# The fifth product of four pairs of steps of a feed-forward layer, computed as seven smaller products and added to its sum by POOL

## The chip, the cores and the metric

The kernel runs on one core of a Trainium2 chip. The metric is the device time of one execution in microseconds; the kernel before took 848.61 us in the median of three runs (847.42 to 848.70).

## The reference

The program computes an attention whose mask comes from hash buckets of the queries and keys, and then a feed-forward block on its output. The change is in the first layer of that block, `h = x @ w_in`:

```python
n_tokens, d_model, d_ff = (3072, 512, 2048)

def _moe_ref(x, w_in, w_out) -> np.ndarray:
    h = x @ w_in
    g = h * (1.0 / (1.0 + np.exp(-1.702 * h)))
    return (g @ w_out).astype(np.float32)
```

## The kernel before

**The tiling.** x is held transposed (`xT`), so the first layer's output has d_ff on the partitions. The layer is computed by Strassen's scheme in Winograd's form: instead of eight products of quarters there are seven, of sums of quarters. `quarters_in` gives the seven left factors (quarters of w_in and their sums in `s_in`), `quarters_x` the seven right ones (quarters of x and their sums in `t_x`); `LEFT` and `RIGHT` say which belong to products 1 to 7. A step takes 128 rows of each half of d_ff and a block of 1,024 tokens (`sb`, three of them). Each of its seven products has 128 x 256 times 256 x 512, two matmuls of 512 columns; eight steps make a block, 24 the layer. In the trace each such fp32 matmul is two records.

**Pairs.** Steps 2 to 21 run in pairs t = 1 to 10 (`pair_of_steps(t)`, steps 2t and 2t+1; t // 4 is the block). Two steps together give a product of 256 x 256 times 256 x 512, which can be split by the same scheme once more ("nested"): seven matmuls of 128 x 128 times 128 x 256 take the place of four of 512 columns. Before the change this is done for products 2, 4 and 3 (`TWICE`), and products 1, 6, 5 and 7 are done whole, as `p1`, `p6`, `p5`, `p7`, once for each of the two steps. `nested` returns five pieces (`one` to `five`, with 1, 2, 1, 2 and 1 of the seven matmuls); each piece leaves a PSUM half bank (`at`) that DVE then adds into the tile concerned (`into`). The factors of a nested product are sums of sums: `nest_w` makes the left ones, `nest_x` the right ones, all on POOL. The results of the pair stand in four tiles u, v, c21 and c22 of 128 x 1,024. There are two sets of them, one for odd t and one for even t; a new tile of a set takes the place of that of t - 2.

**The order.** PE, DVE, ScalarE (ACT) and POOL each work strictly in the order written out. A pair has eight slots, one for each of its whole products in `order`. Work that is to come later is put down with `plan(t, at, ...)`, for slot `at` of pair t (from 9 on: slot `at - 8` of the next pair, from 17 on of the one after), and `play` brings it behind the slot's product: first what was planned with `small=True` (the pieces of nested products), then the rest. So in every slot the pieces come first. Product 2's pieces into u are planned from slot 3, product 3's into v from slot 4 (its second piece in slot 6), product 4's into c21 from slot 9 (its fourth and fifth pieces in slots 7 and 8 of the next pair).

**What else is planned.** `g_part`: four sums of the second layer's input (lines 230 to 233) on POOL, in slots 12, 13, 14 and 17; the last reads c21 and c22. `todo`: the conversion of w_out from its 64-bit form, in six steps on DVE (L188, L190, L196, L201, L205, L208), with a square on ACT (L198) and a load on ACT's queue; two steps each in slots 2, 3 and 4 for step 2t, two each in slots 6 and 7, one in 8 and one in 9 for step 2t+1, as far as there are conversions. `low`: the sums over a part of w_out in the last pair, t = 10, three on POOL (L222, L224, L225) and one on DVE (L223), which overwrites what the first one reads. Product 5 before the change: `p5(i)` is a product of two matmuls into the bank "b", added to v by DVE (L919) and copied to c22 by ACT (L1035); `p7(i)` goes on in the bank of `p1` and `p6`, and DVE adds it to c22 (L919), ACT copies it to c21 (L1040). There are two banks "a", one for each step of a pair; the next pair's first product needs the first of them.

Of the kernel before, what the change touches and what calls it, by code (L numbers as in the profile page):

```python
# [38 lines left out]
def kernel(  # L39
# [806 lines left out]
    def feed_forward(tag, late=()):  # L846
# [9 lines left out]
        with ExitStack() as fctx:  # L856
# [75 lines left out]
            X = {}  # L932
            TWICE = (2, 4, 3)

            def nest_w(t):
                sums = {}
                m = slice(2 * t * P, (2 * t + 2) * P)
                for o in TWICE:
# [3 lines left out]
                    new = w_out_sb[:, t - 2, 12:16, :] if (o, n) == (4, 4) else nest.tile([P, n, P], F32, name=f"w{o}{t}")  # L942
                    new = [new[:, i] for i in range(n)]
                    s3 = x[2] if n == 3 else new[3]
                    W[o, t] = [x[0], x[1], s3, x[3]] + new[0:3]
                    sums[o] = sums_a(nc.gpsimd, x[0], x[1], s3, x[3], *new[0:3], a21=x[2])
                return sums

            def nest_x(sb, rooms):
                sums = {}  # L950
                rooms = list(rooms)
                for o in (2, 3, 4):
# [4 lines left out]
                    sums[o] = [lambda a=t1, b=b12, c=b11: nc.gpsimd.tensor_tensor(a, b, c, op=Alu.subtract),  # L957
                               lambda a=t2, b=b22, c=t1: nc.gpsimd.tensor_tensor(a, b, c, op=Alu.subtract),
                               lambda a=d12, b=b22, c=b12: nc.gpsimd.tensor_tensor(a, b, c, op=Alu.subtract),
                               lambda a=t4, b=b21, c=t2: nc.gpsimd.tensor_tensor(a, b, c, op=Alu.subtract)]  # L960
                return sums

            def nested(o, sb, t, tiles, name, bank_of, done):
# [10 lines left out]
                def into(x, first):  # L974
                    dst = tiles[name][:, first * TH : first * TH + x.shape[-1]]
                    add(dst, x, dst)

                def one():
                    ps[0] = bank_of()
                    into(go(1, True), 0)  # L980

                def two():
                    go(6)
                    go(2)
                    into(ps[0], 0)

                def three():
                    into(go(7), 3)

                def four():  # L990

                    x, y = go(4), go(5, True)
                    into(x, 2)
                    into(y, 3)

                def five():
# [15 lines left out]
            def pair_of_steps(t):  # L1012

                sb, m0 = divmod(2 * t, MT)
                tiles, a = {}, [None, None]

                def place(name, i):
                    if name not in tiles:
# [10 lines left out]
                    nc.scalar.copy(place("v", i), a[i])  # L1029

                def p5(i):
                    b = outer_bank("b")
                    product(b, sb, m0 + i, 5)
                    add(place("v", i), b, place("v", i))
                    nc.scalar.copy(place("c22", i), b)  # L1035

                def p7(i):
                    product(a[i], sb, m0 + i, 7, False)
                    add(place("c22", i), a[i], place("c22", i))
                    nc.scalar.copy(place("c21", i), a[i])  # L1040
                    if i:
                        emit(tiles["c22"])
                        keep(sb, m0, 3, tiles["c22"], nc.scalar)

                def done(at):
                    def f(x):
# [20 lines left out]
                for i, at in enumerate((12, 13, 14, 17)):  # L1067
                    for j in range(2):
                        plan(t, at + j, lambda i=i, j=j: g_part(i, j))
                order = (p1, 0), (p1, 1), (p6, 0), (p5, 0), (p6, 1), (p5, 1), (p7, 0), (p7, 1)  # L1070
                for at, (f, i) in enumerate(order, 1):
                    f(i)
                    play(8 * t + at)
# [241 lines left out]
            for f in in_sums(1) + in_sums(2, 2):  # L1315
# [23 lines left out]
            for i in (list(range(1, LATE + 1)) if late else []) + free[:FC]:  # L1339
# [20 lines left out]
            for t in NESTED:  # L1360
# [171 lines left out]
```

## Time and profile before

| | us |
|---|---|
| median of three runs | 848.61 |
| the profiled execution | 848.2 |
| its span, first to last instruction | 846.4 |
| PE busy | 836.6 |
| DVE busy | 676.1 |
| POOL busy | 382.8 |
| ACT busy | 337.7 |

The attention runs to 308 us, the first layer to 585 us, the second to the end. Rows of the trace in order of time have the start, the duration, the engine, the line, the operation, what is written and read, and how many records were merged; in brackets stands how long the engine had been idle and what released it. A row of a window has the window, then the busy time of PE, weight loads, DVE, ACT and POOL with counts, the granted clock, and the share and rate of the DMA engines. A row of groups has the number of instructions, their busy time, the mean in ns of one, and the idle time before them.

### The profile page before, as it was taken

The page shows a single profiled execution, that of the slowest core. Times are in us where ns is not written, and L with a number is a line of the kernel's source. Part 1 is how long each engine was busy: PE and PEld are TensorE (multiplying, and loading weights), DVE is VectorE, ACT ScalarE, POOL GpSimd, SP SyncE. Part 2 cuts the span into 40 slices and gives each one's busy share as a digit, 9 for nine tenths or more (in the row PEclk, how much of TensorE's full clock was granted, in tenths as well). Part 3 has the DMA queues.
Part 4 walks back from the last instruction along what each step waited for, and adds up shares of the span by engine and source line. Part 5 has one row for each costly group of instructions (what it writes and reads, how often), then busy time and mean ns, then how long its engine had stood idle before and what let it go on. Part 6 is the DMA issues. An engine that isn't in the chain of part 4 may idle for free.

```text
span 846.4 us, 14968 instructions
## 1 busy us (share of the span) xinstructions
PE 836.6 (99%) x5662; PEld 522.3 (62%) x5662; DVE 676.1 (80%) x1073; ACT 337.7 (40%) x550; POOL 382.8 (45%) x324
## 2 busy tenths in 40 slices
PE   8999999999999999999999999999999999999996
PEld 4444444444444444556666666656888888888885
DVE  6478988887888985785878678848999977797776
ACT  6766766766676634434444344443000000000000
POOL 5433443344344359999844686858865000000000
PEclk9999999999999999999999999999999999999999
DMA  8678887788763105446555546657844685467524
GB/s 142 117 150 142 151 171 132 139 158 153 163 155 96 50 2 173 149 145 229 209 195 199 218 174 224 223 224 249 314 178 166 199 261 199 154 195 249 198 100 101
DMA packets 165341, 144.92 MB, mean 171 GB/s; under 512 B 124112, under 2 KB 140112, under 8 KB 160272
## 3 DMA queue, kind: packets, MB, share of 16 engines
q1 hardware_dynamic: 154352, 110.54, 47.7%
q10 hardware_dynamic: 10912, 33.39, 12.1%
q8 instruction: 45, 0.74, 0.4%
q14 instruction: 32, 0.26, 0.1%
HBM read 79.69 MB, written 50.33 MB: 154 GB/s over the span
## 4 chain that ended last, share of the span: by engine, by line
PE 96%; DVE 2%; issue 1%; POOL 1%; POOLq 0%; DVEq 0%
PE product L1240 28%; PE product L901 22%; PE s L547 15%; PE s L514 15%; PE small L971 7%; PE product L971 4%; PE s L496 2%; PE s L460 1%; PE s L569 1%; DVE t_x L1245 0%; DVE y L1220 0%; DVE t1b L230 0%; DVE raw_g L231 0%; DVE t2b L232 0%; PE s L410 0%
## 5 line engine op out<-in xcount | busy, mean ns | idle before, releaser
L484 ACT ACTIVATE e<-s 128x768 f32<-128x768 f32 x192 | 143.3, 811 | 49.2 <-PE s L514 44.3
L547 PE MATMUL s<-e,v 128*32 128x385 f32 x1536 | 130.9, 488 | 0.0
L525 POOL TENSOR_TENSOR t_x<-e 128x768 f32<-128x768 f32 x32 | 61.1, 1910 | 136.1 <-ACT e L484 121.6
L901 PE MATMUL product<-xT,w_in_sb 128*128 128x512 f32 x208 | 96.8, 592 | 0.0
L547 PEld LDWEIGHTS s<-e,v 128*32 128x32 f32 x1536 | 46.7, 109 | 79.3 <-issue 62.8
L901 PE MATMUL product<-t_x,s_in 128*128 128x512 f32 x192 | 89.8, 593 | 0.0
L514 PE MATMUL s<-s_in 32*128 32x384 f32 x912 | 87.9, 481 | 0.0
L525 POOL TENSOR_TENSOR t_x<-t_x,e 128x768 f32<-128x768 f32 x32 | 55.3, 1727 | 43.3 <-ACT e L484 41.8
L538 DVE TENSOR_TENSOR acc<-acc,e 128x768 f32<-128x768 f32 x63 | 70.9, 1126 | 2.3
L1276 ACT COPY wide<-product 128x256 f32<-128x256 f32 x20 | 7.4, 372 | 158.2 <-PE product L1240 125.0
L901 PEld LDWEIGHTS product<-xT,w_in_sb 128*128 128x128 f32 x208 | 39.4, 190 | 31.8 <-issue 28.9
L514 PEld LDWEIGHTS s<-s_in 32*128 32x128 f32 x912 | 43.9, 185 | 23.3 <-issue 2.2
L901 PEld LDWEIGHTS product<-t_x,s_in 128*128 128x128 f32 x192 | 36.4, 190 | 28.3 <-issue 25.6
L919 DVE TENSOR_TENSOR u<-product,u 128x256 f32<-128x256 f32 (+1 forms) x64 | 29.8, 478 | 23.2 <-PE product L971 20.9
L514 PE MATMUL s<-own 32*128 32x384 f32 x432 | 44.3, 482 | 0.0
L465 DVE TENSOR_SCALAR f<-s,above,weight 128x384 bf16<-128x384 f32 x15 | 10.1, 676 | 36.5 <-PE s L569 23.6
L230 POOL TENSOR_TENSOR u<-v,u 128x1024 f32<-128x1024 f32 (+1 forms) x12 | 26.2, 2182 | 20.8 <-ACT v L916 15.6
L919 DVE TENSOR_TENSOR c<-small,c 128x256 f32<-128x256 f32 (+1 forms) x60 | 26.9, 461 | 9.7 <-PE small L971 9.5
L535 DVE SCALAR_TENSOR_TENSOR acc<-t_x,e 128x768 f32<-128x768 f32 x31 | 29.3, 945 | 6.3 <-POOL t_x L525 3.5
L919 DVE TENSOR_TENSOR v<-small,v 128x256 f32<-128x256 f32 (+1 forms) x60 | 27.1, 466 | 8.5 <-PE small L971 6.0
L1035 ACT COPY c<-product 128x512 f32<-128x512 f32 x20 | 11.7, 586 | 51.9 <-DVE v L919 44.8
L1240 PE MATMUL product<-s_in,xT 128*128 128x256 f32 x136 | 31.3, 379 | 0.0
(302 smaller groups left out, 1808.8 us busy)
## 6 DMA issues: line engine op xcount, KB each, us to landing
raw_g<-g_dram SPq DMA_DIRECT2D x20, 1024.0 KB, 6.1
s_in<-g_dram SPq DMA_DIRECT2D x18, 1024.0 KB, 5.1
g_dram<-c ACTq DMA_DIRECT2D x20, 512.0 KB, 3.1
raw<-in_moe_w_out_dram ACTq DMA_DIRECT2D x16, 512.0 KB, 3.7
raw<-in_moe_w_in_dram ACTq DMA_DIRECT2D x15, 512.0 KB, 5.8
s_in<-own SPq DMA_DIRECT2D x36, 192.0 KB, 4.7
v<-in_v_dram SPq DMA_DIRECT2D x16, 384.0 KB, 4.2
g_dram<-u ACTq DMA_DIRECT2D x10, 512.0 KB, 2.9
```

What stands on the lines that cost most here:

```text
L230: return [lambda: eng.tensor_tensor(t1, b12, b11, op=Alu.subtract), lambda: eng.tensor_tensor(b12, b22, b12, op=Alu.subtract), lambda: eng ...
L484: nc.scalar.activation(es[c][:, kt, :, 0:HS], ps[:, :, 0:HS], Act.Exp, scale=1.0 / D**0.5)
L496: nc.tensor.matmul(ps[:, j, 0:HS], a[hs, keys], m[hs, cols], start=at == 0, stop=at == 1)
L514: nc.tensor.matmul(ps[i][:, j, 0:HS], a[r0 : r0 + 32, keys], m[r0 : r0 + 32, cols], start=at == 0, stop=at == 2)
L525: nc.gpsimd.tensor_tensor(low_sum, low_sum if i else e[:, 0], e[:, i + 1], op=Alu.add)
L535: nc.vector.scalar_tensor_tensor(acc, terms[0], T * TINY, terms[1], op0=Alu.add, op1=Alu.add)
L538: nc.vector.tensor_tensor(acc, acc, terms[i + 1], op=Alu.add)
L547: nc.tensor.matmul(av[D * j + d : D * j + d + 32, :], vt[:, j, row, d : d + 32], es[c][:, t, j, :], start=(t == 0), stop=(t == T - 1))
L901: nc.tensor.matmul(ps, wq[LEFT[i]][:, kc, :], xq[RIGHT[i]][:, kc, :], start=(start and kc == 0), stop=(kc == K2 - 1), skip_group_check=not ...
L919: nc.vector.tensor_tensor(dst, x, y, op=Alu.add)
L971: nc.tensor.matmul(x, wq[LEFT[i]], xq[RIGHT[i]], start=start, stop=True, skip_group_check=True)
L1240: nc.tensor.matmul(ps, wq[LEFT[i]][:, c, :], gq[RIGHT[i]][:, c, :], start=(onto is None and c == 0), stop=(c == F4 - 1), skip_group_check= ...
```

## The change

For t = 5, 6, 9 and 10 (`FIFTH`) product 5 is nested as well. Its first contributions are copied to c22 by ACT (`begin`), the others added by DVE; when all five pieces are through, POOL adds c22 to v, at the head of slot 5's other work. `order` changes, the addition of product 7 to c22 and the gelu and store of c22 come out of `p7` as `p8` and `p9` and stand at the end of slots 7 and 8. The factors get places: the sums of w in a part of w_out's tile, copied from there to `xT` by ACT in pair 8; the sums of x in `xT`, where one place of `spare` (the last g sum's result of pair 5) gives way. The four sums of `low` go to other slots.

```diff
-            def nest_w(t):
+            FIFTH = (5, 6, 9, 10)
+
+            def nest_w(t, which=TWICE):
...
+                    if o == 5:
+                        new = fifth_w[t][0]
...
-            def nest_x(sb, rooms):
+            def nest_x(sb, rooms, which=(2, 3, 4)):
...
+                def begin(x, at):
+
+                    if o == 5:
+                        nc.scalar.copy(tiles[name][:, at * TH : (at + 1) * TH], x)
+                    else:
+                        into(x, at)
+
                 def one():
+                    if name not in tiles:
+                        tiles[name] = staged_pair(name, t % 2 == 1)
                     ps[0] = bank_of()
-                    into(go(1, True), 0)
+                    begin(go(1, True), 0)
 
                 def two():
                     go(6)
                     go(2)
-                    into(ps[0], 0)
+                    if o == 5:
+                        into(ps[0][:, 0:TH], 0)
+                        begin(ps[0][:, TH:], 1)
+                    else:
+                        into(ps[0], 0)
 
                 def three():
-                    into(go(7), 3)
+                    begin(go(7), 3)
 
                 def four():
 
                     x, y = go(4), go(5, True)
-                    into(x, 2)
+                    begin(x, 2)
                     into(y, 3)
...
                 def p5(i):
+                    if fifth:
+                        return
...
                 def p7(i):
                     product(a[i], sb, m0 + i, 7, False)
+                    if not fifth:
+                        p8(i)
+                    nc.scalar.copy(place("c21", i), a[i])
+                    if i and not fifth:
+                        p9()
+
+                def p8(i):
                     add(place("c22", i), a[i], place("c22", i))
-                    nc.scalar.copy(place("c21", i), a[i])
-                    if i:
-                        emit(tiles["c22"])
-                        keep(sb, m0, 3, tiles["c22"], nc.scalar)
+
+                def p9():
+                    emit(tiles["c22"])
+                    keep(sb, m0, 3, tiles["c22"], nc.scalar)
...
+                if fifth:
+                    order = (p1, 0), (p1, 1), (p6, 0), (p6, 1), (p5, 0), (p5, 1), (p7, 0), (p7, 1)
+                    for i, f in enumerate(nested(5, sb, t, tiles, "c22", lambda: outer_bank("b"), lambda x: None), 1):
+                        plan(t, i, f, small=True)
+                    plan(t, 5)
+                    agenda[8 * t + 5][1].insert(0, lambda: nc.gpsimd.tensor_tensor(tiles["v"], tiles["v"], tiles["c22"], op=Alu.add))
+                    plan(t, 7, lambda: p8(0))
+                    plan(t, 8, lambda: p8(1), p9)
...
-                      for k, i in ((3, 0), (2, 0), (3, 0), (3, 1))]
+                      for k, i in ((3, 0), (3, 0), (3, 0), (3, 1))]
...
+            fifth_w = {1: [w_out_sb[:, 0, 12:15, :]], 2: [w_out_sb[:, 0:3, 11, :]]}
+            for i, x in fifth_w.items():
+                x.append(xT[:, i - 1, 2 * XT : 2 * XT + 3 * P].rearrange("p (n d) -> p n d", d=P))
+            fifth_x = {1: [xT[:, 2, i * TH : (i + 1) * TH] for i in range(4)],
+                       2: [xT[:, 2, 2 * j * XT + i * TH : 2 * j * XT + (i + 1) * TH] for j in range(2) for i in range(2)]}
...
+                if t + 1 in FIFTH and (5, t % (MT // 2) + 1) not in W:
+                    plan(t, 7, *nest_w(t % (MT // 2) + 1, (5,))[5])
+                if t in FIFTH and (5, sb) not in X:
+                    agenda.setdefault(8 * t + 1, ([], []))[1][0:0] = nest_x(sb, fifth_x[sb], (5,))[5]
+                if t == MT:
+
+                    for i, (old, new) in fifth_w.items():
+                        plan(t, 1, lambda old=old, new=new: nc.scalar.copy(new, old))
+                        W[5, i][4:] = [new[:, j] for j in range(3)]
                 if t + 1 == NESTED.stop:
-                    for i, f in zip((1, 5, 2, 3), low):
+                    for i, f in zip((6, 8, 7, 8), low):
                         plan(t, i, f)
```

More of the change, by code (lines that the diff above doesn't have):

```diff
@@ L933, in feed_forward @@
             TWICE = (2, 4, 3)
-            def nest_w(t):
+            FIFTH = (5, 6, 9, 10)
+            def nest_w(t, which=TWICE):
                 sums = {}
                 m = slice(2 * t * P, (2 * t + 2) * P)
-                for o in TWICE:
+                for o in which:
                     w = quarters_in(m)[LEFT[o]]
@@ L941, in nest_w @@
                     n = 3 if t < 3 else 4
-                    new = w_out_sb[:, t - 2, 12:16, :] if (o, n) == (4, 4) else nest.tile([P, n, P], F32, name=f"w{o}{t}")
+                    if o == 5:
+                        new = fifth_w[t][0]
+                    else:
+                        new = w_out_sb[:, t - 2, 12:16, :] if (o, n) == (4, 4) else nest.tile([P, n, P], F32, name=f"w{o}{t}")
                     new = [new[:, i] for i in range(n)]
@@ L947, in nest_w @@
                 return sums
-            def nest_x(sb, rooms):
+            def nest_x(sb, rooms, which=(2, 3, 4)):
                 sums = {}
                 rooms = list(rooms)
-                for o in (2, 3, 4):
+                for o in which:
                     b = quarters_x(sb)[RIGHT[o]]
@@ L984, in two @@
                     go(2)
-                    into(ps[0], 0)
+                    if o == 5:
+                        into(ps[0][:, 0:TH], 0)
+                        begin(ps[0][:, TH:], 1)
+                    else:
+                        into(ps[0], 0)
                 def three():
-                    into(go(7), 3)
+                    begin(go(7), 3)
                 def four():
                     x, y = go(4), go(5, True)
-                    into(x, 2)
+                    begin(x, 2)
                     into(y, 3)
@@ L1015, in pair_of_steps @@
                 tiles, a = {}, [None, None]
+                fifth = t in FIFTH
                 def place(name, i):
```

## The prediction

> **What bounds the kernel now.** I read the page first: the busy shares and the chain that ended last.
>
> ```profile
> PE 836.6 (99%) x5662; PEld 522.3 (62%) x5662; DVE 676.1 (80%) x1073; ACT 337.7 (40%) x550; POOL 382.8 (45%) x324
> PE 96%; DVE 2%; issue 1%; POOL 1%; POOLq 0%; DVEq 0%
> ```
>
> TensorE carries nearly the whole chain. A busy PE can still be a waiting one, so next come PE's rows in order of time for the first pair that changes, t=5 ("pair 5"), and the busy time of the stretch behind.
>
> ```profile
> 423.25 0.59 PE L971 MATMUL product<-xT,w 128*128 128x256 f32 x2
> ...
> 427.99 1.88 PE L901 MATMUL product<-t_x,s_in 128*128 128x512 f32 x4
> 429.71 0.59 PE L971 MATMUL small<-xT,s_in 128*128 128x256 f32 x2
> 430.14 1.88 PE L901 MATMUL product<-t_x,s_in 128*128 128x512 f32 x4
> 440.46 0.59 PE L971 MATMUL small<-t_x,w 128*128 128x256 f32 x2
> 441.32 1.88 PE L901 MATMUL product<-xT,w_in_sb 128*128 128x512 f32 x4
> 620.00:700.00 80.00, 79.80 (x370) 69.95 (x369) 73.08 (x115) 5.22 (x14) 22.66 (x16) 1.00 0.62 206
> ```
>
> Starts follow one another at a fixed pace: 427.99 to 429.71 is 1.72 us for a whole product (512 columns, four records), 429.71 to 430.14 is 0.43 us for a nested one (256 columns, two records). A pair holds 8 x 1.72 + 21 x 0.43 = 22.8 us, so pair 5, which ends at 441.32, began at 418.52, with no gap. Layer two is as full (79.80 of 80 us). So PE's stream is the time: every gap opened in it is paid in full.
>
> **The products.** Two whole products, 3.44 us, give way to seven nested ones, 3.01 us: 0.43 us saved a pair, **-1.72 us** for four. Each pair's PE work becomes 22.36 us. In us from its start, as the new order puts it: first piece of the fifth product ends 3.44, second runs 6.45 to 7.31, fourth ends 14.19, last 15.91; the second piece of product 3 (into v) 16.77; the fourth of product 4 (into c21) 19.35, its fifth starts 21.50; next pair 22.36.
>
> **The wait on v.** POOL's new add reads all of c22 and writes all of v. DVE's next add into v, the second piece of product 3, must wait for it, and DVE works in order. The rows of today behind that place, and POOL's price:
>
> ```profile
> 423.88 0.42 DVE L919 TENSOR_TENSOR u<-product,u 128x256 f32<-128x256 f32 x1 [0.52 <-PE product L971]
> ...
> 431.15 0.68 DVE L205 TENSOR_TENSOR bits<-bits,part 128x512 f32<-128x512 f32 x1
> 431.93 1.08 DVE L208 SCALAR_TENSOR_TENSOR w_out_sb<-size,bits 128x512 f32<-128x512 f32 x1
> 432.86 0.41 DVE L919 TENSOR_TENSOR c<-small,c 128x256 f32<-128x256 f32 x1
> 435.93 0.69 DVE L919 TENSOR_TENSOR v<-small,v 128x512 f32<-128x512 f32 x1
> 436.54 0.68 DVE L188 TENSOR_SCALAR part<-raw 128x512 uint32<-128x512 uint32 x1
> 437.26 0.69 DVE L190 SCALAR_TENSOR_TENSOR bits<-raw,part 128x512 uint32<-128x512 uint32 x1
> 437.86 0.69 DVE L919 TENSOR_TENSOR c<-product,c 128x512 f32<-128x512 f32 x1
> 438.51 0.76 DVE L919 TENSOR_TENSOR c<-small,c 128x256 f32<-128x256 f32 x2
> 439.19 0.41 DVE L919 TENSOR_TENSOR u<-product,u 128x256 f32<-128x256 f32 x1
> 439.52 0.68 DVE L196 TENSOR_SCALAR part<-bits 128x512 uint32<-128x512 uint32 x1
> 440.24 0.69 DVE L201 SCALAR_TENSOR_TENSOR part<-raw,part 128x512 f32<-128x512 uint32 x1
> 440.84 0.68 DVE L919 TENSOR_TENSOR c<-product,c 128x512 f32<-128x512 f32 x1
> 428.51 2.36 POOL L230 TENSOR_TENSOR u<-v,u 128x1024 f32<-128x1024 f32 x1 [2.83 <-ACT v L916]
> ```
>
> From start to start on a full queue: 0.60 for an add of 512 from PSUM, 0.33 for one of 256 (439.19 to 439.52), 0.72 for L188 and L196, 0.60 for L190 and L201, 0.78 for L205, 0.93 for L208. A result is taken up 0.2 after PE (423.25 + 0.43 against 423.88). So from the pair's start: fourth piece's add 14.4, L205 14.7, L208 15.5, c21 16.4, u 16.8, last piece's add 17.4 to 17.8. POOL is idle by then (its g sum for u is done) and adds 17.85 to 20.2. DVE takes up v at 20.25; today it does at 435.93 - 418.52 = 17.4. Behind it: L188 20.85, L190 21.55, the two c21 adds 22.15 to 22.9, u 22.8, L196 23.15, L201 23.85, the moved c22 add (`p8(0)`) 24.45 to 25.15. PE waits there twice: the fifth piece of product 4 writes the half bank that the second c21 add reads (22.95 for 21.50, 1.45 us), and the next pair's first product needs the bank that `p8(0)` reads (25.2, 1.4 us more). **+2.85 us** for pairs 5, 6 and 9, **+8.55**. Pair 10 has no conversion (L188 to L201) there: DVE is through at 22.6, **+0.2**.
>
> **The place of c22.** Its first write moves from the fourth slot to the first. There are two c22 tiles, one for odd pairs; the last g sum of two pairs before (L233) reads the old one, and stands in the same slot behind the new piece. ScalarE's copy must wait for it.
>
> ```profile
> 421.25 0.73 POOL L958 TENSOR_TENSOR w_out_sb<-t_x,w_out_sb 128x256 f32<-128x256 f32 x1
> 421.94 2.37 POOL L233 TENSOR_TENSOR w_out_sb<-c,c 128x1024 f32<-128x1024 f32 x1
> 424.27 0.73 POOL L959 TENSOR_TENSOR w_out_sb<-t_x 128x256 f32<-128x256 f32 x1
> 424.95 0.73 POOL L960 TENSOR_TENSOR w_out_sb<-t_x,w_out_sb 128x256 f32<-128x256 f32 x1
> 513.14 2.36 POOL L233 TENSOR_TENSOR xT<-c,c 128x1024 f32<-128x1024 f32 x1
> 524.88 1.27 POOL L222 TENSOR_TENSOR xT<-w_out_sb 128x512 f32<-128x512 f32 x1
> 528.69 1.27 POOL L225 TENSOR_TENSOR xT<-w_out_sb,xT 128x512 f32<-128x512 f32 x1
> L1276 ACT COPY wide<-product 128x256 f32<-128x256 f32 x20 | 7.4, 372 | 158.2 <-PE product L1240 125.0
> L222 POOL TENSOR_TENSOR w<-w_in_sb 128x128 f32<-128x128 f32 x7 | 3.2, 458 | 0.0
> ```
>
> In pair 5 four new sums of x, 0.7 us apart (424.27 to 424.95), go ahead of that L233: it runs 424.75 to 427.1, the copy (0.37) to 427.55, and the second piece, due at 418.52 + 6.45 = 424.97, starts at 427.6: **+2.6**. Pair 9 stands alike (513.14 is 3.4 after its start, as 421.94 is): **+2.6**. Pair 6: POOL does the add to 20.2 of pair 5, two g sums, four w sums (0.46 each), L233 to 29.3, which is 4.1 of pair 6: nothing. Pair 10: the sums of w_out (four, 1.27 each from 524.88) stand between, so L233 ends at 7.3 and the copy at 7.7, for 6.45: **+1.3**.
>
> **The low sums of w_out.** They move from slots 1, 5, 2, 3 of pair 10 to 6, 8, 7, 8.
>
> ```profile
> 538.21 2.37 POOL L222 TENSOR_TENSOR xT<-w_out_sb 128x1024 f32<-128x1024 f32 x1
> 547.95 3.35 DVE L223 TENSOR_TENSOR w_out_sb<-w_out_sb 128x1024 f32<-128x1024 f32 x1
> 547.87 2.35 POOL L231 TENSOR_TENSOR v<-c,v 128x1024 f32<-128x1024 f32 x1
> 550.30 3.23 POOL L232 TENSOR_TENSOR c<-c,u 128x1024 f32<-128x1024 f32 x1
> 575.37 1.22 DVE L222 TENSOR_TENSOR xT<-w_out_sb 128x1024 f32<-128x1024 f32 x1
> ```
>
> L223 overwrites what L222 reads. Today L222 is through long before. In the new order L222 comes behind POOL's add (to 20.2) and two g sums (2.4 each, 547.87 to 550.30), 25.05 to 27.4 of pair 10, and DVE stands still from about 23 until then. L223 runs 27.45 to 30.8; behind it wait `p8(1)` and the next step's adds into u (done 32.15), and PE, due to write their bank at 27.3, waits **+4.9**. With L223 at 1.22, the row of the same size with POOL idle, it is 2.8; I take 3.35, since POOL will be adding beside it. Neither can turn into a gain: the wait ends with POOL's row.
>
> **The rest, at nothing.** ACT loses two copies of 512 a pair for four of 256, and copies two 128x384 tiles in pair 8 (between 0.37 and 0.59 each); ACT is 40% busy, and without that cover they cost 1 us. The last sum's store in pair 5 goes to a place that is written every pair (22.8 us apart) instead of every other; its store lands in a few. The c22 store on ACT's queue moves behind c21's, and nothing on PE's path waits for it. The w sums fill POOL's idle 3.69 us of pair 4 (row below); uncovered, 1.9.
>
> ```profile
> 420.13 1.05 POOL L957 TENSOR_TENSOR w_out_sb<-t_x 128x256 f32<-128x256 f32 x1 [3.69 <-DVE t_x L233]
> ```
>
> **Sum**: -1.72 + 8.55 + 0.2 + 2.6 + 2.6 + 1.3 + 4.9 = +18.4. The profiled execution took 848.2 (span 846.4 and 1.8 around it), so 866.6; the median, 848.61, lies 0.4 higher. I forecast **867.0**.
>
> **The rivals.** *The clock drops in the new gaps.* When PE ended at 839.4 its granted clock held 1.00 until about 844.5:
>
> ```profile
> 843.40:844.40 1.00, 0.00 (x0) 0.00 (x0) 0.00 (x0) 0.00 (x0) 0.00 (x0) 1.00 0.14 40
> 845.40:846.40 1.00, 0.00 (x0) 0.00 (x0) 0.00 (x0) 0.00 (x0) 0.00 (x0) 0.50 0.00 0
> ```
>
> My longest gap, 4.9, is just short of these 5. If it halves the clock, and that lasts as long as it took to fall, 5 us pass at half pace: +2.5, 869.5. The Trainium skill ("TensorE: Matmul & The Clock Gate", Part 1) has the array at half clock after one idle window of about 3.4 us, and the window runs free of the kernel. By that rule the gap of 4.9 could be enough and 2.6 could not; the trace's 5 us fits a window that had to begin after PE's end.
>
> *The copy into c22 waits for nothing*, if the old tile's last reader doesn't hold the new one. Without 6.5: 860.5. For it speaks that no such wait stands in the trace; against it, that the reader comes later in the program and would read overwritten data.
>
> *Only the wait on v counts*: without the 4.9 too, if the move of the low sums finds DVE's queue empty enough: 855.6. Against it stands L222, which can't come ahead of POOL's g sums.
>
> *Faster*: DVE absorbs the add. PE loses nothing if v is taken up by 17.4, as today; from there `p8(0)` ends 4.9 later, at 22.3, when the bank is due. That needs POOL's 2.36 hidden before 17.4, a start by 15, while the last piece leaves PE at 15.91. Should it hold, and c22 and the low sums be harmless, only the -1.72 stays: 846.9. The change not doing what it says (seven products as slow as eight) is excluded by 0.43 against 1.72.
>
> **How the numbers follow.** A measurement of this kernel can tell about 0.2%, 1.7 us, from no change. Forecast 0.57, clock 0.10, copy free 0.14, v alone 0.10, faster 0.09. Only the last touches the bound: half of it counts as faster, half as the same; slower holds 0.91. The range runs from below the third rival, 855, to 872, above the clock and with some room for restarts after some ten gaps; it leaves out the last and a tail.
>
> **What would show it.** In the new profile: two gaps on PE in pairs 5, 6 and 9, at the fifth piece of product 4 and at the next pair's first product, with DVE's v add waiting for POOL 2.5 to 3 us; an ACT copy into c22 waiting for L233 in pairs 5, 9 and 10; L223 on DVE waiting for POOL behind pair 10; PE gap-free elsewhere, layer two unmoved. If PE has no gaps in these pairs, I am wrong in the main; if `p8(0)` runs before L196, by 1.4 us a pair.

## The result, and the profile after

The changed kernel takes 873.26 us in the median of six runs (869.91 to 875.54), beside 848.4 for the kernel before in the same job: a ratio of 1.0289, 95% interval 1.0267 to 1.0312. Slower, as forecast, but 1.3 us above the upper end of the range and 6 above the forecast. The profiled execution took 873.55 us, its span 871.7, that is 25.3 longer than before.

The busy shares and the chain that ended last, of the kernel after:

```profile
PE 845.3 (97%) x5686; PEld 531.5 (61%) x5686; DVE 670.5 (77%) x1077; ACT 338.9 (39%) x560; POOL 400.3 (46%) x344
...
PE 32%; POOL 2%; DVE 2%; issue 2%; DMA 1%; ACT 0%; DVEq 0%; ACTq 0%; POOLq 0%
```

PE got less work (28 matmuls of 256 columns for 16 of 512), yet its busy time grew by 8.7 us, and its share of the span fell from 99 to 97%. So PE both stands still and runs slower somewhere. Its waits between 400 and 620 us (who waits for whom, us in total, times, longest):

```profile
PE product L976 <- ACT c L986: 6.3, 3, 2.5
PE small L976 <- DVE c L919: 5.3, 4, 1.7
PE product L901 <- DVE c L919: 3.4, 3, 1.1
PE product L976 <- DVE u L919: 2.3, 1, 2.3
```

Before, there were none. The four lines are the three waits of the forecast: the copy into c22, the wait on v with its two places, and the low sums. Rows of the kernel after in order of time show each (line 976 is the matmul of a nested product, 986 the copy of `begin`, 1104 POOL's add of c22 to v):

```profile
425.16 2.34 POOL L233 TENSOR_TENSOR w_out_sb<-c,c 128x1024 f32<-128x1024 f32 x1
427.54 0.37 ACT L986 COPY c<-product 128x256 f32<-128x256 f32 x1 [4.35 <-POOL w_out_sb L233]
427.96 0.70 PE L976 MATMUL product<-xT,w_out_sb 128*128 128x256 f32 x2 [2.46 <-ACT c L986]
...
439.84 2.35 POOL L1104 TENSOR_TENSOR v<-v,c 128x1024 f32<-128x1024 f32 x1 [4.61 <-issue]
441.42 1.88 PE L901 MATMUL product<-xT,w_in_sb 128*128 128x512 f32 x4
442.23 0.69 DVE L919 TENSOR_TENSOR v<-small,v 128x512 f32<-128x512 f32 x1 [2.52 <-POOL v L1104]
444.96 0.70 PE L976 MATMUL small<-t_x,w 128*128 128x256 f32 x2 [1.67 <-DVE c L919]
445.50 0.59 PE L976 MATMUL small<-xT,s_in 128*128 128x256 f32 x2
447.21 3.37 PE L901 MATMUL product<-xT,w_in_sb 128*128 128x512 f32 x4 [1.12 <-DVE c L919]
450.38 0.95 PE L976 MATMUL product<-xT,w_in_sb 128*128 128x256 f32 x2
451.16 0.59 PE L976 MATMUL product<-xT,w 128*128 128x256 f32 x2
...
552.64 2.36 POOL L232 TENSOR_TENSOR c<-c,u 128x1024 f32<-128x1024 f32 x1
555.02 0.32 SPq L911 DMA_DIRECT2D g_dram<-c  x1
555.07 2.35 POOL L233 TENSOR_TENSOR s_in<-c,c 128x1024 f32<-128x1024 f32 x1
559.53 0.37 ACT L986 COPY c<-product 128x256 f32<-128x256 f32 x1 [3.92 <-DMA g_dram<-c]
...
581.26 1.22 DVE L223 TENSOR_TENSOR w_out_sb<-w_out_sb 128x1024 f32<-128x1024 f32 x1 [4.05 <-POOL xT L222]
581.31 3.40 POOL L224 TENSOR_TENSOR xT<-xT,w_out_sb 128x1024 f32<-128x1024 f32 x1
583.81 0.87 PE L976 MATMUL product<-xT,w 128*128 128x256 f32 x2 [2.26 <-DVE u L919]
```

The first three are the copy into c22 in pair 5: POOL's last g sum, then ACT, then PE, 2.46 us late. The next block is the wait on v. Then comes what the forecast has not: the product at 447.21 runs until the next start at 450.38, 3.17 us for 1.72, and the pieces behind it 0.78 for 0.43. That is the clock. Windows of the kernel after, cut at a spacing of 3.41 us, show it in the granted clock (the column behind the five busy times):

```profile
444.26:447.67 3.41, 1.59 (x5) 0.98 (x6) 3.38 (x8) 0.64 (x2) 3.25 (x4) 1.00 0.45 159
447.67:451.08 3.41, 3.41 (x6) 1.60 (x5) 1.35 (x3) 2.39 (x3) 3.33 (x4) 0.50 0.90 252
451.08:454.50 3.42, 3.42 (x13) 2.25 (x13) 2.04 (x4) 0.67 (x3) 0.07 (x1) 1.00 1.03 420
```

For exactly one such window the clock is at half. This happens four times: behind the wait on v of pairs 5, 6 and 9 (at 447.7, 475.0, 550.1) and behind the low sums (584.2). From start to start, less the pace of the rows before, the gaps and the slow stretches add up so, beside the terms of the forecast:

| term | forecast | measured, us |
|---|---|---|
| seven products for eight | -1.72 | not separable here |
| wait on v, pairs 5, 6, 9 and 10 | 8.75 | 3.2 + 3.2 + 3.2 + 0.5 = 10.1 |
| place of c22, pairs 5, 9, 10 | 6.5 | 2.6 + 2.6 + 1.5 = 6.7 |
| low sums | 4.9 | 2.4 |
| the clock at half | 0 | 4 x 1.75 = 7.0 |
| sum | 18.4 | 24.5 with the -1.72 (span: 25.3) |

0.4 of the missing 0.8 us stands ahead of pair 5. The row of the clock is the one that decides, and the first experiments go there.

### The profile page after: what moved, and what is told of

Its sections match the earlier page's. It is cut to its first block, busy times and chain, and to the rows that moved or that the text cites. A ratio compares the mean times of both kernels' runs of the same rounds, so it can differ in the third digit from the quotient of the medians.

```text
span 871.7 us, 15046 instructions
## 1 busy us (share of the span) xinstructions
PE 845.3 (97%) x5686; PEld 531.5 (61%) x5686; DVE 670.5 (77%) x1077; ACT 338.9 (39%) x560; POOL 400.3 (46%) x344
## 5 line engine op out<-in xcount | busy, mean ns | idle before, releaser
L901 PE MATMUL product<-xT,w_in_sb 128*128 128x512 f32 x208 | 101.6, 617 | 3.4 <-DVE c L919 3.4
L901 PE MATMUL product<-t_x,s_in 128*128 128x512 f32 x160 | 75.5, 597 | 0.0
L901 PEld LDWEIGHTS product<-t_x,s_in 128*128 128x128 f32 x160 | 30.8, 193 | 24.4 <-issue 22.4
L465 DVE TENSOR_SCALAR f<-s,above,weight 128x384 bf16<-128x384 f32 x15 | 10.1, 676 | 38.7 <-PE s L569 23.6
L919 DVE TENSOR_TENSOR c<-product,c 128x512 f32<-128x512 f32 (+1 forms) x36 | 21.4, 596 | 20.4 <-ACT u L1044 5.8
```

The lines of the kernel that those rows point to most:

```text
L901: nc.tensor.matmul(ps, wq[LEFT[i]][:, kc, :], xq[RIGHT[i]][:, kc, :], start=(start and kc == 0), stop=(kc == K2 - 1), skip_group_check=not ...
L919: nc.vector.tensor_tensor(dst, x, y, op=Alu.add)
```

## The experiments

**The clock: PE kept busy in the gaps.** Small products of zeros (one bf16 matmul of 512 columns, 0.22 us) go into an idle bank at the end of pairs 5, 6 and 9: six ahead of product 4's fifth piece and four ahead of the next pair's first product (x_fill), or the four alone (x_fill2).

```diff
+                def fill(count):
+                    ps = outer_bank("b")
+                    for _ in range(count):
+                        nc.tensor.matmul(ps, idle[:, 0:P], idle, start=True, stop=True)
...
+                    if at == 8 and t in (5, 6, 9) and 6:
+                        fill(6)
                     play(8 * t + at)
+                if t in (5, 6, 9) and 4:
+                    fill(4)
```

> The changed kernel with ten matmuls more at the end of pairs 5, 6 and 9, on constant zeros into the idle bank b: six ahead of the fifth piece of product 4, four ahead of the next pair's first product, where PE waits 1.67 and 1.12 us. They are in no result. Theory (the clock halves because PE is idle for more than half of a stretch of about 3.4 us, and the first products behind the gaps then take 3.2 instead of 1.7 us): the ends of the two gaps stay, the granted clock is 1.00 behind them, and three times 1.8 us go: 873.3 - 5.4 = 868. Rival (the products behind a gap are slow for another reason, such as transfers or a restart after a wait): the first product still takes 3.2 us, and the time stays within 1 us of 873 or rises by what the extra matmuls don't hide.

> As the last, but only the four matmuls ahead of the next pair's first product: the first gap of 1.67 us stays. Theory (a share of a stretch counts, not one gap): with some 0.9 us of idle time taken out of the last stretch before the clock falls, less than half of it is idle, so the clock stays 1.00 here too and the time is as with ten, 868. Rival (the longer gap of 1.67 us sets the clock back by itself): first products at 3.2 us as before, 873.

Measured: 871.84 (ratio 1.0279, 1.0262 to 1.0296) and 871.78 (1.0278, 1.0260 to 1.0295). The end of pair 5 in x_fill2:

```profile
445.57 0.70 PE L976 MATMUL small<-t_x,w 128*128 128x256 f32 x2 [1.66 <-DVE c L919]
...
446.54 1.03 PE L1110 MATMUL product<-idle 128*128 128x512 bf16 x4
447.83 1.98 PE L901 MATMUL product<-xT,w_in_sb 128*128 128x512 f32 x4 [0.26 <-DVE c L919]
449.65 0.59 PE L976 MATMUL product<-xT,w_in_sb 128*128 128x256 f32 x2
```

The product behind the gap now takes 1.82 us to the next start and not 3.17, at the same wait for DVE: the slow product was the clock. But the time fell by only 1.5 us. In both runs the clock now fell behind the gaps of the copy into c22 instead (in x_fill at 427.65, 530.05 and 560.77). Those of pairs 5 and 9, 2.46 us, had done no harm in the kernel after; that of pair 10 had grown from 1.35 to 3.06. So a gap of the same length drops the clock or not. In x_fill the three falls lie 30.0 and 39.0 times 3.413 us behind the first, in the kernel after 8.0, 30.0 and 40.0 times: a fixed grid.

**What drops the clock.** Into the kernel before, which has no gaps, 18 were put behind slots 2 and 8 of pairs 1 to 9: a product of zeros, copies of its bank by ACT, a product that reads the copy. First with 2 to 5 copies (x_gaps), then with two at each place (x_gaps2).

```diff
+                    if (t, at) in counts:
+                        ps = outer_bank("b")
+                        nc.tensor.matmul(ps, idle[:, 0:P], idle, start=True, stop=True)
+                        for _ in range(counts[t, at]):
+                            nc.scalar.copy(idle, ps)
+                        ps = outer_bank("b")
+                        nc.tensor.matmul(ps, idle[:, 0:P], idle, start=True, stop=True)
```

> The kernel before, with 18 gaps put into PE's stream of pairs 1 to 9 (behind slots 2 and 8): a small product of zeros, then 2, 3, 4 or 5 copies of its bank by ACT one behind the other, then a product that reads the copy. Gaps of about 1.4, 1.9, 2.4 and 2.9 us are due, 38 us in all, and 8 us for the 36 small products. Theory (the granted clock is judged at the end of each stretch of a fixed grid of 3.41 us and falls to 0.50 for the next one if PE stood over about 1.8 us of it): no fall behind the 5 shortest, some 8 falls of 3.41 us among the other 13, by their place on the grid, each costing up to 1.7: about 908 us. Rival 1 (a whole stretch has to be empty): no fall at all, 894 us. Rival 2 (any gap over 1.8 us drops the clock, wherever it lies): 13 falls, about 916 us.

> The kernel before with the same 18 gaps, but two copies at each place: all between 2.0 and 2.6 us (those with two copies were 1.6 to 2.1 in the run of mixed lengths, none of which dropped the clock, while all of 3.4 and more did). Theory (half of a stretch of the fixed grid of 3.41 us, some 1.8 us idle in it, decides): gaps of one length drop the clock at some places and not at others, about half of the 18, and each fall stands where over 1.8 us of the stretch before it were idle: 848 + 38 + 8 + 9 x 1.7 = 909 us, between 903 and 916. Rival 1 (a gap has to be longer than some 2.6 to 3.4 us): no fall, 894 us. Rival 2 (the length alone decides, at some 2.1 us): all or nearly all fall, 920 us and more.

Measured: 960.69 and 945.77 us, one run each, far above all the forecasts, since the copies stood in ACT's queue behind its other work (in one place of x_gaps the product of zeros ran at 388.29 and the first copy at 391.94): the gaps were 1.6 to 6.4 us and 1.6 to 4.5. The totals therefore decide nothing; the places do. In the first run the clock fell behind 13 gaps, all those of 3.36 us and more, and behind none of the four of 2.13. In the second it fell behind 16, among them six of the seven that have the same 2.13 us. Two of its gaps, on the grid:

```profile
430.89:434.30 3.41, 1.28 (x6) 0.56 (x5) 2.12 (x5) 2.23 (x3) 0.00 (x0) 1.00 0.38 154
434.30:437.71 3.41, 3.41 (x6) 1.64 (x5) 0.00 (x0) 0.49 (x1) 0.00 (x0) 0.50 0.01 2
...
362.62:366.03 3.41, 1.54 (x8) 0.92 (x6) 2.44 (x5) 2.61 (x4) 3.25 (x6) 1.00 0.16 66
366.03:369.44 3.41, 3.15 (x11) 2.04 (x12) 0.45 (x2) 0.91 (x3) 3.33 (x8) 1.00 0.24 93
```

The first row of each two holds a gap of 2.13 us. One lies wholly inside its stretch, and the next stretch runs at half clock; the other ends 0.26 us into the next stretch, and nothing falls. The busy column gives a piece 0.59 us where its pace is 0.43, so idle time is better counted from start to start: 2.29 us here in the first, 2.03 in the second, 2.09 in the window 444.26:447.67 of the kernel after. Counted so over all runs with gaps, for stretches at full clock: of 37 that were idle for 1.2 to 2.0 us none is followed by a fall, of the 45 idle for more than 2.17 all are, and of ten between 2.00 and 2.16 five. Both rivals fall (neither a whole empty stretch nor the length of a gap alone decides), and the theory's threshold of 1.8 us becomes 2.0 to 2.2.

**The wait on v: what DVE waits for.** x_order takes the wait's cause away: the second piece of product 3 is played one slot later (behind POOL's add), and the adds into c22 go ahead of the conversions. x_dve keeps the order and lets DVE add c22 to v.

```diff
-                    for i, f in zip((0, 2, 4, 6, 7), nested(o, sb, t, tiles, name, bank_of, done(at))):
+                    for i, f in zip((0, 3 if fifth and o == 3 else 2, 4, 6, 7), nested(o, sb, t, tiles, name, bank_of, done(at))):
...
-                    plan(t, 7, lambda: p8(0))
-                    plan(t, 8, lambda: p8(1), p9)
+                    plan(t, 8, p9)
+                    for i in range(2):
+                        plan(t, 7 + i)
+                        agenda[8 * t + 7 + i][1].insert(0, lambda i=i: p8(i))
```

> The changed kernel with the second piece of product 3 in slot 7 instead of 6 of the four pairs, so that DVE's add into v stands behind the conversions and the c21 adds, and with the adds of product 7 to c22 ahead of slot 7's and 8's conversions; POOL's add as it is. Theory (DVE standing still for POOL's add is what opens the two gaps in pairs 5, 6 and 9): both gaps close to under 0.2 us and with them the half clock: 3 x (3.2 + 1.8) = 15 us less. POOL's work then is late against PE by what PE gained, so ACT's copy into c22 waits longer in pair 10, 2 to 3 us more: 873.3 - 15 + 2.5 = 861. Rival (POOL's add itself, on a shared resource, slows DVE or PE wherever it stands): no more than 5 us less, 868.

```diff
-                    agenda[8 * t + 5][1].insert(0, lambda: nc.gpsimd.tensor_tensor(tiles["v"], tiles["v"], tiles["c22"], op=Alu.add))
+                    agenda[8 * t + 5][1].insert(0, lambda: nc.vector.tensor_tensor(tiles["v"], tiles["v"], tiles["c22"], op=Alu.add))
```

> The changed kernel with the add of c22 to v on DVE and not on POOL. Theory (the wait on v is POOL's 2.35 us between the last piece's add and DVE's next add into v): DVE does the add itself in about 1.2 us, so the place of the next v add comes some 1.1 us earlier in pairs 5, 6, 9: 3.2 becomes 2.0 to 2.2 us of gaps in each, and 0.5 becomes nothing in pair 10. The longest of these gaps is then under 1.5 us and the clock does not fall behind them (three times 1.8 less): 873.3 - 3.3 - 0.5 - 5.4 = 864 us. Rival (DVE's own queue is the bound, and an operation more on it costs what POOL's cost): 3.2 us of gaps in each as before, 872 to 874 us.

Measured: x_order 865.77 us (ratio 1.0224, 1.0203 to 1.0246), x_dve 863.76 (1.0187, 1.0171 to 1.0202). The total of x_dve is the one expected, 864, but in part by luck: its gaps at v shrank by 2.2 us and not by 3.8, and two falls of the clock were left and not one; in return the waits for the low sums (2.4) and for pair 10's copy (1.5), which were to stay, are gone. In x_dve the same two places of PE and the add, by DVE itself:

```profile
441.09 1.44 DVE L1104 TENSOR_TENSOR v<-v,c 128x1024 f32<-128x1024 f32 x1
...
445.37 0.70 PE L976 MATMUL small<-t_x,w 128*128 128x256 f32 x2 [0.74 <-DVE c L919]
...
447.62 1.98 PE L901 MATMUL product<-xT,w_in_sb 128*128 128x512 f32 x4 [1.13 <-DVE c L919]
```

The first wait falls from 1.67 to 0.74, by what POOL's 2.35 us are longer than DVE's 1.44, the second stays (1.13 for 1.12), and the clock falls twice (behind a copy at 428.6, and at 473.0) and not four times. So it is the add between DVE's two adds into v that PE pays for, at its duration. In x_order the end of pair 5 has no gap, pair 6 a new one, and pair 10 a huge one:

```profile
442.87 0.59 PE L976 MATMUL small<-t_x,w 128*128 128x256 f32 x2
443.30 0.59 PE L976 MATMUL small<-xT,s_in 128*128 128x256 f32 x2
443.73 1.88 PE L901 MATMUL product<-xT,w_in_sb 128*128 128x512 f32 x4
...
452.11 0.70 PE L976 MATMUL product<-xT,w_out_sb 128*128 128x256 f32 x2 [1.76 <-ACT c L986]
...
544.39 2.35 POOL L232 TENSOR_TENSOR c<-c,u 128x1024 f32<-128x1024 f32 x1
546.76 0.32 SPq L911 DMA_DIRECT2D g_dram<-c  x1
...
552.05 1.22 PE L976 MATMUL product<-xT 128*128 128x256 f32 x2 [6.58 <-ACT c L986]
```

All of the wait on v is gone, but some 5 us come back in pair 10, where 2 to 3 had been expected, with a halved clock for two stretches (PE works in only half of that time, so it loses some 1.8 us); 1.9 us come back in pair 6, where nothing had been expected. These are most of the way from 861 to 866. The rows say why: c22 of pair 10 takes the tile of pair 8, and the third g sum of pair 8 (L232) leaves its result there to be stored. L232 stands behind POOL's four sums of w_out (1.23 each), its store is issued at 546.76 and the copy can start when it has landed. From POOL's add in pair 9 on, this chain runs without a gap, so it comes no earlier when PE gains time behind that add: what PE gains at the end of pair 9 (3.2 us of waits and 1.75 of the clock) it waits out in pair 10. In pair 6 the copy waits for the same kind of store.

**The place of c22: the x sums earlier.** The four sums of x ahead of L233 in pairs 5 and 9 go to slot 7 of the pair before.

```diff
-                if t in FIFTH and (5, sb) not in X:
-                    agenda.setdefault(8 * t + 1, ([], []))[1][0:0] = nest_x(sb, fifth_x[sb], (5,))[5]
+                if t + 1 in FIFTH and (5, sb) not in X:
+                    plan(t, 7, *nest_x(sb, fifth_x[sb], (5,))[5])
```

> The changed kernel with the four sums of x for the fifth product in slot 7 of pairs 4 and 8 instead of ahead of the last g sum in slot 1 of pairs 5 and 9. Theory (ACT's copy into c22 waits for that g sum, which waits for these four): the gaps of 2.46 us in pairs 5 and 9 go to under 0.3: 873.3 - 5 = 868.3. Rival (the copy waits for the old c22 whatever stands before that sum, or for the sums of x themselves): no change, 873.

Measured: 868.50 us (1.0247, 1.0230 to 1.0264): the total as expected, its parts not quite. In the profiled execution, the shortest of the four (866.39), the gap of pair 9 closed, that of pair 10 shrank to 0.2, and that of pair 5 only halved:

```profile
420.83 1.18 POOL L965 TENSOR_TENSOR xT<-t_x,xT 128x256 f32<-128x256 f32 x1
...
423.46 2.36 POOL L233 TENSOR_TENSOR w_out_sb<-c,c 128x1024 f32<-128x1024 f32 x1
426.28 0.70 PE L976 MATMUL product<-xT,w_out_sb 128*128 128x256 f32 x2 [1.23 <-ACT c L986]
```

The four sums still run until 422, and two more stand between them and L233 in POOL's queue. The price of this place is what is ahead of L233, as forecast.

**The low sums.** DVE's L223 goes to slot 10.

```diff
-                    for i, f in zip((6, 8, 7, 8), low):
+                    for i, f in zip((6, 10, 7, 8), low):
```

> The changed kernel with one part moved: DVE's low sum of w_out (L223) played in slot 10 of pair 10 and not in slot 8. Theory (the wait of PE behind pair 10 is DVE's queue standing behind L223, which waits for POOL's L222): the gap of 2.26 us at 581.5 closes, and with it the fall of the granted clock at 584.2, worth some 1.8 us: 873.3 - 2.4 - 1.8 = 869.1 us, everything ahead of 575 unchanged. Rival (POOL's low sums themselves are late, wherever DVE's stands: then the wait comes back a few us later, at the first readers of the sums): 872 to 873 us.

Measured: 872.72 us (868.82 to 873.86; 1.0283, 1.0259 to 1.0307), so the total hardly moved. The place itself did what the theory said:

```profile
582.43 1.88 PE L901 MATMUL product<-t_x,s_in 128*128 128x512 f32 x4
584.14 0.59 PE L976 MATMUL product<-xT,w 128*128 128x256 f32 x2
```

No gap, no fall of the clock, and no later wait. But the rest was not unchanged, as the theory had assumed: in this execution the clock fell at 427.8 and 533.6 too, behind the copies, and not in pair 10 any more, where the copy then waited 2.84 us instead of 1.35. Which of the gaps halve the clock differs from execution to execution, so one gap of 2.4 us can't be weighed by a total here.

**Everything together.** x_all2 has the edits of x_order and x_low, POOL's add into v in two halves, the two x sums that the second piece needs ahead of the pair and the other two behind L233, the w sums of pair 6 in POOL's idle time of pair 5, and the sums of w_out behind the g sums, and L233 one slot earlier. x_all4, whose edits are shown beside those of x_order and x_low, puts the third g sum earlier (by setting the halves of the add behind the first and the second one) and L233 back in its slot.

```diff
-                    plan(t, 5)
-                    agenda[8 * t + 5][1].insert(0, lambda: nc.gpsimd.tensor_tensor(tiles["v"], tiles["v"], tiles["c22"], op=Alu.add))
+                    for at, i in ((4, 1), (5, 0)):
+                        plan(t, at, lambda i=i: nc.gpsimd.tensor_tensor(place("v", i), place("v", i), place("c22", i), op=Alu.add))
...
-                    for i, f in enumerate(more[4]):
-                        plan(t, 8 + i // 2, f)
+                    fifth_sums = nest_x(sb, fifth_x[sb], (5,))[5]
+                    plan(t, 8, *fifth_sums[:2])
+                    plan(t, 9, *more[4][:2], fifth_sums[2], *more[4][2:], fifth_sums[3])
...
-                    plan(t, 5, *inner_sums(0))
+                    plan(t, 9, *inner_sums(0))
...
-                    plan(t, 7, *nest_w(t % (MT // 2) + 1, (5,))[5])
-                if t in FIFTH and (5, sb) not in X:
-                    agenda.setdefault(8 * t + 1, ([], []))[1][0:0] = nest_x(sb, fifth_x[sb], (5,))[5]
+                    plan(t, 3 if t in FIFTH else 7, *nest_w(t % (MT // 2) + 1, (5,))[5])
```

> The changed kernel, with every wait that was found met by an order of its own: the second piece of product 3 a slot later, the adds into c22 ahead of the conversions, POOL's add into v in two halves, the last g sum of a pair one slot earlier, the two x sums that the second piece needs at the end of the pair before and the other two behind, the w sums of pair 6 in POOL's idle time of pair 5, the sums of w_out for layer two one pair's beginning later, L223 in slot 10. Theory (the change costs its four waits and the clock behind them, and nothing else): no gap over 0.3 us on PE in pairs 5 to 10 and no fall of the clock, 846.7 to 848.5 us, that is the kernel before less up to 1.7 us. Rival (POOL's queue has no room for the fifth product, and each order only moves the wait to another place): two or more gaps of over 1 us left, 852 us or more.

> The kernel of the last run of this kind with its five leftover gaps met too: the last g sum of a pair back in its old slot, ahead of it only the two x sums that the second piece needs, and POOL's two halves of the add into v behind the first and the second g sum rather than ahead of them, so that the third g sum, whose store out of the old c22 tile ends some 4.6 us after it, comes 2.4 us earlier. Theory (the waits and the clock behind them are all that the change costs): that run's gaps, 0.9 + 1.2 + 2.0 + 0.8 + 2.3 us, and its one fall of the clock, 1.7 us, are gone: 855.0 - 8.9 = 846.1, say 846.0 to 848.0 us, 0.1 to 0.3% under the kernel before. Rival (POOL and the stores behind it have no room, so that an order only moves the wait): a gap of over 1 us stays in pair 6 or 10, 849 us or more.

Measured: x_all2 855.01 us (1.0077, 1.0063 to 1.0091): as its rival has it, with five gaps of 0.6 to 2.0 us and one fall of the clock. Its longest is again the store:

```profile
539.04 0.32 SPq L911 DMA_DIRECT2D g_dram<-c  x1
544.67 0.37 ACT L986 COPY c<-product 128x256 f32<-128x256 f32 x1 [3.06 <-DMA g_dram<-c]
545.10 0.70 PE L976 MATMUL product<-xT 128*128 128x256 f32 x2 [2.00 <-ACT c L986]
```

x_all4: **846.35 us** (845.88 to 846.73, eleven runs) beside 847.72 for the kernel before, ratio 0.9984, 0.9975 to 0.9993. Its busy times:

```profile
PE 835.5 (99%) x5686; PEld 527.6 (62%) x5686; DVE 671.7 (80%) x1077; ACT 338.9 (40%) x560; POOL 400.6 (47%) x348
```

The first layer from pair 5 on, and the beginning of the second, as one window of x_all4:

```profile
418.50:610.00 191.50, 191.50 (x676) 127.94 (x675) 150.18 (x252) 75.70 (x117) 146.72 (x91) 1.00 0.63 226
```

PE is busy for the whole window at the full clock. The fifth product then gives 1.4 us, between 0.6 and 2.1, where the forecast's term was 1.72; all that the change costs beside it is order.

**The clock alone.** Last, the changed kernel with zeros in all its long gaps: the ten at the pair ends, ten ahead of the second piece in pairs 5, 9 and 10, nine behind pair 10.

```diff
+                def zeros(ps, count):
+                    for _ in range(count):
+                        nc.tensor.matmul(ps, idle[:, 0:P], idle, start=False, stop=True, skip_group_check=True)
...
+                if t in (5, 9, 10):
+                    plan(t, 2, lambda: zeros(a[0], 10), small=True)
```

> The changed kernel with small products of zeros (bf16, 512 columns, 0.22 us each) in all its long gaps: 6 and 4 at the end of pairs 5, 6 and 9 as in the first such run, 10 ahead of the second piece of the fifth product in pairs 5, 9 and 10 (added to a bank that its reader has left), 9 ahead of the piece of product 2 behind pair 10. The waits stay what they are; only PE does not stand still in them. Theory (the gaps alone account for the change, and what is over them is the clock's fall): the clock stays at 1.00 from pair 5 on, the copy into c22 of pair 10 waits about 3 us, as in the runs where the clock held ahead of it, and the time is 847.7 - 1.7 + 10.0 (v) + 8.3 (c22) + 2.4 (low sums) = 866.7, between 866 and 868 us; the clock is then the 6 us or so to 873.3. Rival (the zeros cost what the clock gives, or the waits are themselves longer at a slow clock): 870 us or more with the clock at 1.00.

Measured: 870.46 us (869.94 to 873.34; 1.0265, 1.0247 to 1.0284), by the total on the rival's side. The profiled execution was the longest of the four, 873.34 us. In it the clock stayed at 1.00 through pairs 5 to 9 and fell once, in pair 10, where ten zeros did not reach:

```profile
552.55 0.32 SPq L911 DMA_DIRECT2D g_dram<-c  x1
...
559.00 0.37 ACT L986 COPY c<-product 128x256 f32<-128x256 f32 x1 [5.85 <-DMA g_dram<-c]
559.42 0.70 PE L976 MATMUL product<-xT 128*128 128x256 f32 x2 [2.69 <-ACT c L986]
```

From the store's issue to the copy it took 6.4 us here, beside 4.5 in the kernel after, and PE waited through 2.15 us of zeros and 2.7 more. In this execution the zeros cost nothing (what follows them starts when DVE or ACT release it). So one wait did get longer where the clock held. Pair 10's copy waits 1.5 us behind the fall at 550 in the kernel after, and 3.0 in x_fill, x_fill2 and x_low, which had no fall there: the store sets its time, and what PE loses just ahead comes out of the wait. Of the 7.0 us of slow stretches the changed kernel therefore pays some 5.5 (7.0 less 1.5); by this run's total it is 2.8, with the longer store in it.

The mean granted clock of every execution was recorded, and a step at half clock takes 0.002 from it (half of 3.41 in some 870 us). In x_fill3 it is 0.996 for the profiled execution and 0.998 for the other three (869.94 to 870.53 us), as in x_all4, where nothing fell (0.997 to 0.999). So these three had no fall and still stood over the theory's 866.7 by more than 3 us; whether longer waits or the zeros themselves make up the rest is not shown. In the kernel after it goes from 0.994 in the shortest execution (869.91) to 0.988 in the longest (875.54), that is from some two falls to some five: the falls set much of its spread.

## Why the prediction was right and wrong

- **The failed step: the clock, left out of the sum.** The text had: "My longest gap, 4.9, is just short of these 5", and gave the fall a chance of 0.10 and a price of 2.5, once, for the longest gap only. It read the 5 us from PE's end to the fall as the length a gap must have. The runs put another rule in its place: PE's time is judged in fixed stretches of 3.41 us, and one that is idle for over 2.0 to 2.2 halves the next. The 5 us fit it: between 844.40 and 845.40 of the kernel before the mean granted clock is 0.59, so the fall came at 844.58; the stretch before it began at 841.17, and PE, which ended at 839.4, had left only 1.8 us of the one before that idle. By that rule gaps of 2.46 us, or two of 1.67 and 1.12 close together, are enough. The clock fell four times for some 1.75 us each, never behind a gap of over 2.5. The other terms missed by +1.35, +0.2 and -2.5 us; that these nearly cancel is luck, and it leaves the miss of 6 us about equal to the clock's 7.0. What the falls cost in the total stays open between 2.8 us (x_fill3) and these 7.0. The Trainium skill ("TensorE: Matmul & The Clock Gate", Part 1) has the clock at half after one idle window of about 3.4 us, and the window runs free of the kernel. The grid of 3.413 us agrees with the free-running window; a wholly idle window, as the forecast read it, was not needed: 444.26:447.67 was idle for 2.09 us, and the next one ran at half.
- **The wait on v: right in both places and in its order, 10.1 for 8.75.** Product 4's fifth piece was due at 441.42 + 1.72 = 443.14, by the forecast 21.50 after the pair's start; POOL's add at 439.84 then began 18.2 us after it, not 17.85, and these 0.35 us make 3.2 out of 2.85, three times. In pair 10 it is 0.5 for 0.2. DVE's operations ran in the listed order, the moved c22 add behind L196 and L201. x_dve and x_order show the term's cause.
- **The place of c22: right in pairs 5 and 9 (2.6 each), right in size but not in cause in pair 10.** There L233 ended at 557.4 and the copy began at 559.53, when the store of the third g sum had landed. The forecast looked at POOL's last reader of the old tile and forgot the DMA that reads it too. With that the 1.5 us were a coincidence: 6.6 in x_order.
- **The low sums: the wait was where it should be, half as long, 2.4 for 4.9.** L223 took 1.22, not 3.35. The bound of 2.8 that was worked out with 1.22 was the right end; the row from pair 10 of the kernel before was taken as the nearer one. POOL was adding beside it, as the forecast had said, but here POOL's add began 0.05 us later (581.31) and was the one that took longer, 3.40 us beside 2.35. In the kernel before POOL's began first (547.87, 2.35 us), and DVE's, at 547.95, took 3.35.
- **The products**: x_all4 bears out the 0.43 us a pair (1.72 in all) within its interval of 0.6 to 2.1 us.
- **The rivals** *copy free*, *v alone* and *faster* are excluded by the waits. With one fall less, 871.5, the time would lie in the range.

## What to carry to other kernels

A gap on a full PE is not paid at its length: add the chance of a halved stretch behind every place where some 2 us of idle time can fall within 3.4 us, and count two short gaps close together as one. When a tile is written earlier than before, ask for every reader of the old one, the stores among them; and when a wait is set by another queue's chain, time won ahead of it is only waited out there. A change that costs 3% by its waits can be worth 0.16% once each piece has its place.

## What the runs showed of the hardware

- The granted clock falls on a grid of 3.413 us (falls of one execution lie 8.0, 30.0 and 40.0 or 21.0 or 9.0, 13.0, 20.0 and 23.0 steps apart), to 0.50, for one step where the next stretch holds up to some 0.6 us of idle time, for two where it holds 0.84 or more. A stretch at full clock brings a fall when over 2.0 to 2.2 us of it are idle; what decides between 2.00 and 2.16 us of idle time stays open: five stretches fell, five did not.
- A fall moves with the execution: the gap of 2.46 us ahead of the c22 copy in pair 5 was harmless in the kernel after and halved the clock in x_fill, x_fill2, x_low and x_dve. The times of kernels with such gaps spread over 2 to 6 us (869.91 to 875.54), while x_all4, with none, spread over 0.9; x_dve, with two such gaps, spread over 0.3 all the same.
- From the issue of the store of 512 KB out of the c22 of pair 8 to the copy that waited for it, 4.5 us (x_low) to 6.4 us (x_fill3) passed.
- Where a 128x1024 add of DVE and one of POOL overlapped, the one that began first kept its time (POOL 2.35 us at 547.87 of the kernel before, DVE 1.22 at 581.26 of the kernel after) and the other took over 1 us longer than alone (3.35 and 3.40). These are two places; no run tests it.
